# Low parts of the FFN rounds moved from GpSimd to VectorE, and the second pair started chunk by chunk

## Chip, cores, metric

One core of a Trainium2 chip runs the whole kernel. The metric is the device time of one execution in microseconds; the time of a kernel is the median of its runs.

## What is computed

An mLSTM-style attention over 768 steps for 4 batches and 8 heads, then a mixture-of-experts layer in which each expert takes exactly 384 tokens (chosen greedily over all tokens and experts), then a gated FFN on all tokens. Only the second half matters here:

```python
for e in range(E):                      # 8 experts, 384 tokens each
    mask = assigned == e
    h = np.maximum(x[mask] @ w1[e], 0.0)
    out[mask] = h @ w2[e]
...
a = x @ w_a
b = x @ w_b
return (a * b @ w_out).astype(np.float32)
```

## The kernel before

The attention part takes the first 213 us or so; the change doesn't touch it. Then eight **rounds** follow, one for each expert in the order in which experts fill up. A round has 384 tokens (CAP) and two pairs of products.

- **First pair** (`g1`, `g2`): relu(x w1) in eight blocks of 128 features, then times w2. `g2(f-2)` is issued behind `g1(f)`.
- **Second pair** (`ab`, `outp`): for each of twelve blocks two products with w_a and w_b, evacuated by ScalarE (`at`) and multiplied on VectorE (`gf`), then times w_out. `outp(f-2)` is issued behind `ab(f)`.

Every operand is kept as a high and a low part: ScalarE makes the high part by a copy to fp32r (`w1h`, `w2`, `mh`, `xh`, `yh`), another engine subtracts it from the exact value to get the low part (`w1l`, the tail of `w2`, `ml`, `xl`, `yl`), and TensorE takes three products, high by high, low by high, high by low. Before the change GpSimd makes the low parts of the expert's weights (`split_w`, L906, L915, L917; the first two chunks of round 0 are VectorE's) and of the second pair's product (`ml` at L1098), beside gathers of the tokens (`xg`, L845) and scatters of the results (L1137). VectorE makes the low part of the first pair's product (`ml` at L1036), `gf` (L1093), and the low parts of x and y.

Between these the kernel still **routes**: `route(r)` finds expert r's tokens by five counting steps in sequence. A step compares on VectorE (three `G`, L648), counts on TensorE (24 small matmuls into `rt`, L672), tests on VectorE (`okb`, L691), sums on TensorE (L694), and sets the next threshold on VectorE (`d`, L700). Routes 1 to 7 run during rounds 0 to 5 or so. In round 0 five **late conversions** of w_a, w_b and w_out run too (`conv`: VectorE L119, L122, L125, then ScalarE, then GpSimd L134, L136, L149; one buffer `mu`).

What sets the order: each engine works its own list in the order in which the program issues it. The method `mm` adds 0.155 to a counter `now` for every matmul and, when a stream's time has come, takes the next piece of one of three generators: routes, the next expert's weights, late conversions. The number in `yield` is how long that stream then rests on that counter (routes after the first rest 1.25 times as long, PAD). So a VectorE piece is issued a set number of matmuls ahead of the TensorE piece that needs it, and if VectorE is later than that, TensorE stands. In round 0 `wdone` counts the weight steps done, and `g1` pulls the weights stream until enough are.

Of the kernel before, what the change touches and what calls it, by code (L numbers as in the profile page):

```python
# [24 lines left out]
DM = H * D  # L25
E = 8
# [17 lines left out]
class Kern:  # L44
# [68 lines left out]
    def conv(self, pool, kind, i, raw, more, nxt):  # L113
        nc = self.nc
        V, P, A = nc.vector, nc.gpsimd, nc.scalar
        words = raw.bitcast(I32).rearrange("p (n two) -> p n two", two=2)
        qi, sg = self.cva
        u = pool.tile([128, CW], I32, tag="ot", name="mu", bufs=1)
        V.tensor_scalar(u, words[:, :, 1], 3, None, op0=OP.logical_shift_left)  # L119
        more()  # L120
        yield 0.5
        V.tensor_tensor(u, u, qi, op=OP.add)  # L122
        yield 0.8
        F = u.bitcast(F32)
        V.tensor_tensor(F, F, sg, op=OP.mult)  # L125
        if kind == "f":
            h, l = self.wh[i], self.wl[i]
            n4, c4 = slice(0, 512), slice(512, 640)

            def fin():  # L130
                A.activation(h[:, 0:4].rearrange("p a b -> p (a b)"), F[:, n4], AF.Copy)
                th, tl = [pool.tile([128, 128], F32R, name=n, bufs=1) for n in ("mth", "mtl")]
                A.activation(th, F[:, c4], AF.Copy)
                P.tensor_sub(l.rearrange("p a b -> p (a b)"), F[:, n4],  # L134
                             h[:, 0:4].rearrange("p a b -> p (a b)").bitcast(F32))
                P.tensor_sub(tl, F[:, c4], th.bitcast(F32))  # L136
                for s in range(2):
                    r = slice(64 * s, 64 * s + 64)
                    nc.sync.dma_start(h[0:64, 4 + s].bitcast(F32), th[r].bitcast(F32))
                    nc.sync.dma_start(h[64:128, 4 + s].bitcast(F32), tl[r].bitcast(F32))  # L140
                nxt()

            yield from self.later(fin)
        else:
            h = self.woh[i].rearrange("p a b -> p (a b)")

            def fin():
                A.activation(h, F, AF.Copy)
                P.tensor_sub(self.wol[i].rearrange("p a b -> p (a b)"), F, h.bitcast(F32))  # L149
                nxt()  # L150

            yield from self.later(fin)
        self.done.add((kind, i))
# [501 lines left out]
    def route(self, r):  # L655
# [32 lines left out]
        def total(cnt, on):  # L688
            okb = rw.tile([128, E], BF, name="okb")
            ok1 = rw.tile([128, 1], BF, name="ok1")  # L690
            V.tensor_scalar(okb, cnt, float(CAP), None, op0=OP.is_ge, op1=OP.max, accum_out=ok1)  # L691
            yield 0.8
            nn = ps.tile([128, 1], F32, name="rt")
            nc.tensor.matmul(nn, on, ok1, start=True, stop=True)  # L694
            yield 0.6
            return nn
# [198 lines left out]
    def split_w(self, r):  # L895
        nc = self.nc
        V, P, A = nc.vector, nc.gpsimd, nc.scalar

        def one(j):
            raw = self.next_raw()  # L900
            h, l = self.w1h[:, j], self.w1l[:, j]
            A.activation(h, raw, AF.Copy)  # L902
            if r == 0 and j < 2:
                yield 1.0
            e = V if r == 0 and j < 2 else P
            e.tensor_sub(l, raw[:, 0:2], h[:, 0:2].bitcast(F32))  # L906
            V.tensor_sub(h[64:128, 2], raw[64:128, 2], h[64:128, 2].bitcast(F32))  # L907
            self.more_raw()
            yield 2.4

        def two(i):
            raw = self.next_raw()
            h = self.w2[:, 2 * i:2 * i + 2, 0:DM]
            A.activation(h, raw, AF.Copy)
            P.tensor_sub(self.w2[:, 2 * i:2 * i + 2, DM:DM + 64], raw[:, :, 256:320],  # L915
                         h[:, :, 256:320].bitcast(F32))
            P.tensor_sub(self.w2[:, 2 * i:2 * i + 2, DM + 64:], raw[:, :, 0:256], h[:, :, 0:256].bitcast(F32))  # L917
            self.more_raw()
            yield 2.4

        st = [one(j) for j in range(4)] + [two(i) for i in range(NF1 // 2)]
        if r == 0:
            st = [st[i] for i in (0, 1, 4, 2, 5, 3, 6, 7)]
            next(st[0])
            yield 0
            next(st[1])
            yield 0
        for k, f in enumerate(st):
            w = sum(f)
            self.wdone = k + 1  # L930
            yield w

    def prep_x(self, r, xg):
        nc, fw, ps = self.nc, self.fw, self.ps
# [53 lines left out]
    def ffn(self):  # L988
# [34 lines left out]
        for r in range(E):  # L1023
# [15 lines left out]
            def g2(f):  # L1039
                hh, hl = hq.pop(f)  # L1040
                w = self.w2[:, f]
                st, sp = f == 0, f == NF1 - 1
                mm(yp[2], w[:, 256:384], hh, start=st, stop=False)
                mm(yp[2], w[:, 256:384], hl, start=False, stop=sp)
                for m in range(2):
                    wh = w[:, m * 128:m * 128 + 128]
                    wl = w[:, DM + 64 + m * 128:DM + 64 + m * 128 + 128]
                    mm(yp[m], wh, hh, start=st, stop=False)
                    mm(yp[m], wl, hh, start=False, stop=False)
                    mm(yp[m], wh, hl, start=False, stop=sp)  # L1050

            for f in range(NF1):
                while r == 0 and self.wdone < (1, 3, 5, 7)[f // 2] + 1:
# [15 lines left out]
                ws[:] = [self.now, self.weights(r + 1)]  # L1069
            yh = fw.tile([128, 3, CAP], F32R, name="yh", bufs=1)  # L1070
            yl = self.ylt
            yb = fw.tile([64, CAP], F32, tag="at", name="yb", bufs=2)
            A.activation(yb, yp[2][64:128], AF.Copy)
            ys = fw.tile([64, CAP], F32, tag="gf", name="ys", bufs=2)
            V.tensor_add(ys, yp[2][0:64], yb)
            for c in range(2):
                self.split_act(yh, yl, c, yp[c])
            self.split_act(yh, yl, 2, ys)

            gq = {}  # L1080
# [2 lines left out]
            def ab(f):  # L1083
                p = [ps.tile([128, CAP], F32, name="ring", bufs=4) for _ in range(2)]
                wh, wl = self.wh[f], self.wl[f]

                for k in range(2):
                    self.proj(p[k], [wh[:, 2 * k + c] for c in range(2)], [wl[:, 2 * k + c] for c in range(2)],
                              wh[:, 4 + k], yh, yl)
                at = fw.tile([128, CAP], F32, name="at", bufs=2)  # L1090
                A.activation(at, p[0], AF.Copy)  # L1091
                gf = fw.tile([128, CAP], F32, name="gf", bufs=2)
                V.tensor_mul(gf, p[1], at)  # L1093
                gh = fw.tile([128, CAP], F32R, name="mh", bufs=3)
                A.activation(gh, gf, AF.Copy)  # L1095
                gl = fw.tile([128, CAP], F32R, name="ml", bufs=3)
                e = V if r + 1 == E and f == NF2 - 1 else nc.gpsimd
                e.tensor_sub(gl, gf, gh.bitcast(F32))  # L1098
                gq[f] = (gh, gl)

            def outp(f, op, gq, rows=(0, 1, 2)):
# [115 lines left out]
```

## Time and profile before

| | us |
|---|---|
| median of 3 runs | 919.73 (919.49 to 921.26) |
| profiled execution, own time | 922.35 |
| its span, first to last instruction | 920.6 |
| rounds begin (first w1 matmul of each) | 243.0, 347.3, 436.2, 523.1, 608.0, 690.1, 765.1, 838.7 |

| engine | busy us | share of span |
|---|---|---|
| TensorE | 830.0 | 90% |
| VectorE | 543.8 | 59% |
| GpSimd | 433.6 | 47% |
| ScalarE | 337.0 | 37% |

The profile is one execution. Busy times of a stretch are to be read against its own length; the granted clock is that of TensorE, 1.0 being its higher level. "Waits" rows say which instruction stood, and for what.

### The profile page before, as it was taken

The page shows a single profiled execution, that of the slowest core. Times are in us where ns is not written, and L with a number is a line of the kernel's source. Part 1 is how long each engine was busy: PE and PEld are TensorE (multiplying, and loading weights), DVE is VectorE, ACT ScalarE, POOL GpSimd, SP SyncE. Part 2 cuts the span into 40 slices and gives each one's busy share as a digit, 9 for nine tenths or more (in the row PEclk, how much of TensorE's full clock was granted, in tenths as well). Part 3 has the DMA queues.
Part 4 walks back from the last instruction along what each step waited for, and adds up shares of the span by engine and source line. Part 5 has one row for each costly group of instructions (what it writes and reads, how often), then busy time and mean ns, then how long its engine had stood idle before and what let it go on. Part 6 is the DMA issues. An engine that isn't in the chain of part 4 may idle for free.

```text
span 920.6 us, 15838 instructions
## 1 busy us (share of the span) xinstructions
PE 830.0 (90%) x5939; PEld 786.8 (85%) x5939; DVE 543.8 (59%) x1188; ACT 337.0 (37%) x660; POOL 433.6 (47%) x456
## 2 busy tenths in 40 slices
PE   4888978995878889979989999999999999999996
PEld 3788867884778879979988998999899999999996
DVE  7778996846676786585477678667764321321211
ACT  4657646520334332333234224223422532432321
POOL 5688895750433573165147317442723633532122
PEclk9989988896799889989998999999999999999999
DMA  6866765621412220130131022021111311200000
GB/s 170 246 193 198 238 199 143 199 75 41 147 51 72 80 79 22 53 84 13 38 89 45 15 80 75 2 94 32 46 52 43 92 36 43 67 8 22 1 1 22
DMA packets 51037, 73.84 MB, mean 80 GB/s; under 512 B 6160, under 2 KB 41360, under 8 KB 50960
## 3 DMA queue, kind: packets, MB, share of 16 engines
q1 hardware_dynamic: 41744, 45.30, 17.7%
q10 hardware_dynamic: 6912, 19.66, 6.6%
q0 software_dynamic: 2304, 7.87, 2.6%
q8 instruction: 47, 0.77, 0.3%
q14 instruction: 30, 0.25, 0.1%
HBM read 63.37 MB, written 7.86 MB: 77 GB/s over the span
## 4 chain that ended last, share of the span: by engine, by line
PE 64%; DVE 16%; POOL 6%; issue 6%; ACT 5%; DMA 2%; SPq 1%; ACTq 0%; DVEq 0%; POOLq 0%
PE ring L970 32%; PE acc L970 20%; DVE G L648 3%; PE rt L672 2%; PE pq L392 2%; DMA qr<-in_qk_dram 2%; PE pv L423 1%; DVE w1h L907 1%; POOL dd L387 1%; DVE gf L1093 1%; PE pg L408 1%; PE pl L482 1%; DVE mu L122 1%; POOL x L460 1%; ACT yh L966 1%
## 5 line engine op out<-in xcount | busy, mean ns | idle before, releaser
L1098 POOL TENSOR_TENSOR ml<-gf,mh 128x384 fp32r<-128x384 f32 x95 | 106.7, 1123 | 266.4 <-ACT mh L1095 266.1
L970 PE MATMUL ring<-yh,wh 128*128 128x384 f32 x576 | 202.3, 351 | 6.4 <-ACT yh L966 4.6
L970 PE MATMUL ring<-yl,wh 128*128 128x384 f32 x576 | 136.9, 344 | 0.0
L970 PE MATMUL ring<-yh,wl 128*128 128x384 f32 x384 | 132.7, 346 | 0.0
L1093 DVE TENSOR_TENSOR gf<-ring,at 128x384 f32<-128x384 f32 x96 | 53.3, 555 | 126.9 <-PE ring L970 122.8
L970 PEld LDWEIGHTS ring<-yh,wh 128*128 128x128 f32 x576 | 111.4, 193 | 13.9 <-ACT yh L966 7.2
L1095 ACT ACTIVATE mh<-gf 128x384 fp32r<-128x384 f32 x96 | 50.5, 526 | 187.0 <-DVE gf L1093 187.0
L648 DVE TENSOR_TENSOR G<-thc,d 128x1024 bf16<-128x1024 int16 (+1 forms) x90 | 110.4, 1245 | 0.4
L970 PEld LDWEIGHTS ring<-yl,wh 128*128 128x128 f32 x576 | 105.6, 193 | 0.1
L970 PE MATMUL acc<-woh,ml 128*128 128x320 f32 x288 | 91.6, 318 | 0.0
L970 PE MATMUL acc<-woh,mh 128*128 128x320 f32 x288 | 90.7, 315 | 0.0
L970 PE MATMUL acc<-wol,mh 128*128 128x320 f32 x288 | 90.4, 314 | 0.0
L970 PE MATMUL acc<-mh,w 128*128 128x384 f32 x320 | 88.9, 340 | 0.0
L1036 DVE SCALAR_TENSOR_TENSOR ml<-ring,mh 128x384 fp32r<-128x384 f32 x64 | 35.5, 557 | 80.3 <-ACT mh L1034 77.1
L1034 ACT ACTIVATE mh<-ring 128x384 fp32r<-128x384 f32 x64 | 31.5, 492 | 133.5 <-PE ring L970 128.9
L1091 ACT ACTIVATE at<-ring 128x384 f32<-128x384 f32 x96 | 46.8, 488 | 80.0 <-PE ring L970 78.3
L970 PEld LDWEIGHTS ring<-yh,wl 128*128 128x128 f32 x384 | 74.4, 194 | 0.0
L906 POOL TENSOR_TENSOR w1l<-raw,w1h 128x512 fp32r<-128x512 f32 x30 | 44.2, 1478 | 51.0 <-ACT w1h L902 51.0
L970 PE MATMUL ring<-xh,w1h 128*128 128x384 f32 x192 | 66.0, 344 | 0.1
L392 PE MATMUL pq<-qr 128*128 128x256 f32 x192 | 56.9, 425 | 9.9 <-DMA qr<-in_qk_dram 5.2
L970 PE MATMUL acc<-ml,w 128*128 128x384 f32 x192 | 65.2, 339 | 0.3 <-DVE ml L1036 0.3
L970 PEld LDWEIGHTS acc<-mh,w 128*128 128x128 f32 x320 | 58.6, 190 | 0.2 <-issue 0.2
(211 smaller groups left out, 1746.8 us busy)
## 6 DMA issues: line engine op xcount, KB each, us to landing
raw<-in_moe_w_dram SPq DMA_DIRECT2D x32, 320.0 KB
raw<-in_moe_w_dram SPq DMA_DIRECT2D x32, 256.0 KB
vk<-in_vk_dram SPq DMA_DIRECT2D x24, 324.0 KB
qr<-in_qk_dram SPq DMA_DIRECT2D x48, 160.0 KB
mraw<-in_wab_dram ACTq DMA_DIRECT2D x12, 640.0 KB
raw<-in_moe_w_dram SPq DMA_DIRECT2D x64, 64.0 KB
og<-in_og_dram ACTq DMA_DIRECT2D x6, 640.0 KB
qr<-in_qk_dram SPq DMA_DIRECT2D x48, 80.0 KB
```

The lines of the kernel that those rows point to most:

```text
L122: V.tensor_tensor(u, u, qi, op=OP.add)
L392: nc.tensor.matmul(pq[:, o:o + 2], qk[:, 4 + hp], qk[:, H + 2 * hp:H + 2 * hp + 2], start=True, stop=True)
L648: self.nc.vector.tensor_tensor(G, self.thc[:, None, 0:nthr].to_broadcast(dims), d[:, i0:i0 + 8, None].to_broadcast(dims), op=op)
L672: nc.tensor.matmul(cnt[0:nthr], Gs[j][:, i], oh[:, 8 * j + i], start=(j + i == 0), stop=(j * 8 + i == NT - 1))
L906: e.tensor_sub(l, raw[:, 0:2], h[:, 0:2].bitcast(F32))
L970: self.nc.tensor.matmul(*a, **k)
L1034: A.activation(hh, p, AF.Relu)
L1036: V.scalar_tensor_tensor(hl, p, 0.0, hh.bitcast(F32), op0=OP.max, op1=OP.subtract)
L1091: A.activation(at, p[0], AF.Copy)
L1093: V.tensor_mul(gf, p[1], at)
L1095: A.activation(gh, gf, AF.Copy)
L1098: e.tensor_sub(gl, gf, gh.bitcast(F32))
```

## The change

Five edits, in `conv`, `route`, `split_w` and `ffn`:

1. The low parts of w1, w2 and of the second pair's product go from GpSimd to VectorE; those of w2 stand in two pieces with a rest of 1.0 between.
2. In the late conversions (one raw buffer, `rawb == 1`) the multiplication by the sign goes from VectorE to GpSimd.
3. Weight steps are no longer issued whole: `yield from f` replaces `sum(f)`, so `wdone` counts a step one piece later.
4. The rest between `okb` and its sum is 1.2 in place of 0.8.
5. The second pair's start: `g2` makes chunks 0 and 1 of its result ahead of chunk 2, ScalarE and VectorE split chunks 0 and 1 first, and the first block's products go by chunks, both halves interleaved, with the short chunk 2 last.

```diff
-        V.tensor_tensor(F, F, sg, op=OP.mult)
+        (P if self.rawb == 1 else V).tensor_tensor(F, F, sg, op=OP.mult)
...
-            yield 0.8
+            yield 1.2
             nn = ps.tile([128, 1], F32, name="rt")
...
-            e = V if r == 0 and j < 2 else P
-            e.tensor_sub(l, raw[:, 0:2], h[:, 0:2].bitcast(F32))
+            V.tensor_sub(l, raw[:, 0:2], h[:, 0:2].bitcast(F32))
...
-            P.tensor_sub(self.w2[:, 2 * i:2 * i + 2, DM:DM + 64], raw[:, :, 256:320],
+            V.tensor_sub(self.w2[:, 2 * i:2 * i + 2, DM:DM + 64], raw[:, :, 256:320],
                          h[:, :, 256:320].bitcast(F32))
-            P.tensor_sub(self.w2[:, 2 * i:2 * i + 2, DM + 64:], raw[:, :, 0:256], h[:, :, 0:256].bitcast(F32))
+            yield 1.0
+            V.tensor_sub(self.w2[:, 2 * i:2 * i + 2, DM + 64:], raw[:, :, 0:256], h[:, :, 0:256].bitcast(F32))
...
-            yield 2.4
+            yield 1.4
...
-            w = sum(f)
+            yield from f
             self.wdone = k + 1
-            yield w
...
-                mm(yp[2], w[:, 256:384], hh, start=st, stop=False)
-                mm(yp[2], w[:, 256:384], hl, start=False, stop=sp)
                 for m in range(2):
...
+                mm(yp[2], w[:, 256:384], hh, start=st, stop=False)
+                mm(yp[2], w[:, 256:384], hl, start=False, stop=sp)
...
+            for c in range(2):
+                self.split_act(yh, yl, c, yp[c])
             yb = fw.tile([64, CAP], F32, tag="at", name="yb", bufs=2)
...
-            for c in range(2):
-                self.split_act(yh, yl, c, yp[c])
             self.split_act(yh, yl, 2, ys)
...
-                for k in range(2):
+                if f == 0:
+                    for c in range(2):
+                        for k in range(2):
+                            mm(p[k], wh[:, 2 * k + c], yh[:, c], start=c == 0, stop=False)
+                            mm(p[k], wl[:, 2 * k + c], yh[:, c], start=False, stop=False)
+                    for c in range(2):
+                        for k in range(2):
+                            mm(p[k], wh[:, 2 * k + c], yl[:, c], start=False, stop=False)
+                    for k in range(2):
+                        mm(p[k], wh[:, 4 + k], yh[:, 2], start=False, stop=False)
+                    for k in range(2):
+                        mm(p[k], wh[:, 4 + k], yl[:, 2], start=False, stop=True)
+                for k in range(2 if f else 0):
...
-                e = V if r + 1 == E and f == NF2 - 1 else nc.gpsimd
-                e.tensor_sub(gl, gf, gh.bitcast(F32))
+                V.tensor_sub(gl, gf, gh.bitcast(F32))
```

VectorE, late in round 0's second pair, around the first counting step of route 2, before (`ta`, `tb`, `k` are small threshold sums, `d` the threshold, `G` the comparison):

```order
L1093 TENSOR_TENSOR gf<-ring,at 128x384
L710 TENSOR_SCALAR ta<-k_3659 128x24
L711 TENSOR_SCALAR tb<-k_3659 128x24
L691 TENSOR_SCALAR okb,ok_3834<-rt 128x8
L700 TENSOR_SCALAR d_3857<-ta,rt 128x24
L704 SCALAR_TENSOR_TENSOR k_3783<-rt,tb 128x24
L648 TENSOR_TENSOR G<-thc,d_3857 128x1024
L1093 TENSOR_TENSOR gf<-ring,at 128x384
```

The same place on VectorE now (w_2440 is the tile `w2`):

```order
L710 TENSOR_SCALAR ta<-k_3667 128x24
L711 TENSOR_SCALAR tb<-k_3667 128x24
L691 TENSOR_SCALAR okb,ok_3844<-rt 128x8
L914 TENSOR_TENSOR w_2440<-raw_3726,w_2440 128x2x64
L917 TENSOR_TENSOR w_2440<-raw_3726,w_2440 128x2x256
L1104 TENSOR_TENSOR gf<-ring,at 128x384
L1108 TENSOR_TENSOR ml<-gf,mh 128x384
L700 TENSOR_SCALAR d_3876<-ta,rt 128x24
L704 SCALAR_TENSOR_TENSOR k_3799<-rt,tb 128x24
L648 TENSOR_TENSOR G<-thc,d_3876 128x1024
```

Between `okb` and `d` there now stand two weight pieces and a `gf` with its `ml` right behind it.

GpSimd in round 0, from the last weight pieces to the second gather, before:

```order
L917 TENSOR_TENSOR w_2440<-raw_2880,w_2440 128x2x256
L134 TENSOR_TENSOR wl_2426<-mu,wh_2425 128x512
L136 TENSOR_TENSOR mtl<-mu,mth 128x128
L149 TENSOR_TENSOR wol_2432<-mu,woh_2431 128x640
L1098 TENSOR_TENSOR ml<-gf,mh 128x384 x3
L134 TENSOR_TENSOR wl_2428<-mu,wh_2427 128x512
```

And now, from the first gather on:

```order
L845 DMA xg<-xd,idx 128x320 x3
L125 TENSOR_TENSOR mu<-mu,msg 128x640
L134 TENSOR_TENSOR wl_2426<-mu,wh_2425 128x512
L136 TENSOR_TENSOR mtl<-mu,mth 128x128
L125 TENSOR_TENSOR mu<-mu,msg 128x640
L149 TENSOR_TENSOR wol_2432<-mu,woh_2431 128x640
L125 TENSOR_TENSOR mu<-mu,msg 128x640
```

The conversions' multiplications (L125) came in; after the five conversions GpSimd holds gathers, scatters and one-element memsets alone.

TensorE where the second pair of round 1 starts, before (chunks are not named: the first five `yh` rows are chunk 0, 0, 1, 1, 2 of one half):

```order
L970 MATMUL acc<-ml,w_2440 128x384
L970 MATMUL ring<-yh,wh_69 128x384
L970 MATMUL ring<-yh,wl_70 128x384
L970 MATMUL ring<-yh,wh_69 128x384
L970 MATMUL ring<-yh,wl_70 128x384
L970 MATMUL ring<-yh,wh_69 128x384
L970 MATMUL ring<-yl,wh_69 128x384 x3
```

And now, from the third of four such `yh` pairs on:

```order
L969 MATMUL ring<-yh,wh_69 128x384
L969 MATMUL ring<-yh,wl_70 128x384
L969 MATMUL ring<-yh,wh_69 128x384
L969 MATMUL ring<-yh,wl_70 128x384
L969 MATMUL ring<-yl,wh_69 128x384 x4
L969 MATMUL ring<-yh,wh_69 128x384 x2
L969 MATMUL ring<-yl,wh_69 128x384 x2
```

Chunk 2 was the fifth matmul behind the last `acc`; now it is the thirteenth.

## Rows read from the trace of the kernel before

**Rows 1.** Busy time by stretch, one per round (0 to 4, then 6); last columns clock, DMA

```profile
243.00:347.30 104.30, 88.93 (x630) 84.12 (x629) 80.92 (x154) 40.40 (x74) 53.77 (x45) 0.89 0.24 72
347.30:436.20 88.90, 82.94 (x615) 78.81 (x615) 58.87 (x124) 27.70 (x54) 35.27 (x35) 0.96 0.15 45
436.20:523.10 86.90, 82.39 (x616) 78.75 (x615) 58.14 (x118) 26.17 (x51) 35.71 (x33) 0.96 0.15 46
523.10:608.00 84.90, 82.03 (x617) 78.34 (x617) 55.50 (x123) 26.52 (x51) 36.53 (x33) 0.98 0.17 51
608.00:690.10 82.10, 80.00 (x614) 76.63 (x614) 58.69 (x123) 26.06 (x51) 37.49 (x33) 1.00 0.19 59
...
765.10:838.70 73.60, 73.21 (x438) 72.23 (x438) 17.43 (x32) 26.41 (x51) 30.66 (x33) 1.00 0.12 37
```

**Rows 2.** What TensorE waited for in rounds 1 to 4: total us, times, longest

```profile
PE rt L672 <- DVE G L648: 8.6, 6, 3.0
PE rt L694 <- DVE okb L691: 4.7, 4, 2.1
PE ring L970 <- ACT yh L966: 1.5, 4, 0.5
```

**Rows 3.** The same for round 0

```profile
PE rt L672 <- DVE G L648: 8.8, 5, 4.2
PE rt L740 <- DVE ok L737: 2.7, 1, 2.7
```

**Rows 4.** VectorE by time: start us, duration; one operation in rounds 0 and 1, one successor

```profile
320.12 0.35 DVE L629 TENSOR_TENSOR e<-e,w 128x192 f32<-128x192 f32 x1
320.38 0.17 DVE L630 TENSOR_SCALAR d<-sg 128x24 int32<-128x24 int32 x1
...
395.89 4.22 DVE L629 TENSOR_TENSOR e<-e,w 128x192 f32<-128x192 f32 x1
```

**Rows 5.** GpSimd by time, around the second of these

```profile
396.37 1.03 POOL L1098 TENSOR_TENSOR ml<-gf,mh 128x384 fp32r<-128x384 f32 x1
397.34 2.54 POOL L906 TENSOR_TENSOR w1l<-raw,w1h 128x512 fp32r<-128x512 f32 x2
```

**Rows 6.** VectorE's groups by shape in round 1: busy us, mean ns, idle before

```profile
L648 DVE TENSOR_TENSOR G<-thc,d 128x1024 bf16<-128x1024 int16 x15 | 20.0, 1336 | 0.0
...
L648 DVE TENSOR_TENSOR G<-thc,rr 128x1024 bf16<-128x1024 int16 x3 | 3.6, 1218 | 0.0
...
L907 DVE TENSOR_TENSOR w1h<-raw,w1h 64x256 fp32r<-64x256 f32 x4 | 2.5, 618 | 2.1 <-ACT w1h L902 2.0
...
L710 DVE TENSOR_SCALAR ta<-k 128x24 int32<-128x24 int32 x1 | 1.2, 1210 | 0.0
...
L711 DVE TENSOR_SCALAR tb<-k 128x24 int32<-128x24 int32 x1 | 0.2, 165 | 0.0
```

**Rows 7.** VectorE's groups from 232 to 245 us, GpSimd idle: moved operations' prices

```profile
L906 DVE TENSOR_TENSOR w1l<-raw,w1h 128x512 fp32r<-128x512 f32 x2 | 1.4, 692 | 0.7 <-ACT w1h L902 0.7
...
L907 DVE TENSOR_TENSOR w1h<-raw,w1h 64x256 fp32r<-64x256 f32 x2 | 0.8, 423 | 0.1
```

**Rows 8.** VectorE by time at the end, where it makes one `ml` itself

```profile
910.20 0.56 DVE L1098 TENSOR_TENSOR ml<-gf,mh 128x384 fp32r<-128x384 f32 x1 [0.59 <-ACT mh L1095]
```

**Rows 9.** Chain of work that ended last: one counting step's 24 matmuls

```profile
344.36 0.60 PE rt L672 x24
```

**Rows 10.** All engines by time where round 6's second pair starts

```profile
788.32 1.02 ACT L962 ACTIVATE yh<-acc 128x384 fp32r<-128x384 f32 x2
...
788.47 0.34 PE L970 MATMUL acc<-ml,w 128*128 128x384 f32 x1
...
790.34 0.44 PE L970 MATMUL ring<-yh,wh 128*128 128x384 f32 x1 [0.33 <-ACT yh L966]
```

**Rows 11.** GpSimd and VectorE by time in round 0's conversions

```profile
280.28 1.56 POOL L149 TENSOR_TENSOR wol<-mu,woh 128x640 fp32r<-128x640 f32 x1 [9.09 <-ACT woh L148]
...
295.55 0.50 DVE L119 TENSOR_SCALAR mu<-mraw 128x640 int32<-128x640 int32 x1 [3.19 <-POOL mtl L136]
```

## The prediction

> **What bounds the kernel now.** I read the busy time by round first [rows 1]. TensorE works 73.21 of 73.60 us in round 6, where no routing is left: that is a round's floor. Rounds 0 to 4, in which routes run, take 104.3, 88.9, 86.9, 84.9 and 82.1 us. The four from 1 to 4 sum to 342.8, which is 48.4 over four floors. Of that 17.5 is honest work: seven sets of 24 counting matmuls a round at 0.60 to 0.65 [rows 9]. TensorE's own waits in these rounds are 8.6 us for `G` and 4.7 us for `okb` [rows 2], both VectorE's; 1.5 us is the second pair's start. The granted clock was 0.96, 0.96 and 0.98 in rounds 1 to 3 [rows 1], which is 3.6 + 3.5 + 1.7 = 8.8 us lost. About 7 us are left over in shorter waits. Round 0 has 8.8 us of waits for `G`, 2.7 for `ok` [rows 3], and a clock of 0.89, some 11.5 us lost [rows 1]. So the routes' comparisons on VectorE end last, though VectorE is busy only 55 to 59 us of these rounds.
>
> Why they are late is in the single operations. The same multiplication takes 0.35 us in round 0 and 4.22 us in round 1 [rows 4]; through the second, GpSimd worked three instructions in a row, from 396.37 to 399.88 [rows 5]. In round 1, fifteen `G` average 1336 ns where three others average 1218, a small `ta` takes 1210 where its neighbour `tb` takes 165, and `w1h` 618 [rows 6] where it takes 423 with GpSimd idle [rows 7]. That makes 15 x 0.12 = 1.8, 3.9, 1.0 and 0.8 us; taking every shape of round 1 in this way I get 10.0 us of VectorE time lost to GpSimd, 10 to 11 in rounds 2 to 4, 19.5 in round 0.
>
> **The change, part by part.**
>
> *Moved to VectorE.* Per round: twelve `ml` at 0.56 [rows 8], 6.7 us; four `w1l` at 0.69 [rows 7], 2.8 us; four large pieces of w2 of the same 512 elements, 2.8 us; four of 128 elements, which the trace lacks: between the 0.17 of a 24-element operation [rows 6] and the 0.42 of 256 [rows 7], I take 0.29, 1.2 us (0.7 to 1.7). Sum 13.4. Beside it, `ml` stands directly behind its `gf`, and ScalarE's copy lies between: VectorE stood 0.59 us there in the one instance there is [rows 8]. Twelve times that is 7.1. So VectorE gets 20.5 us a round and gives back 10: from 58.9 to about 69 in round 1. That fits a round of 78 on the whole, but not evenly. In round 1's third to eleventh `ab` I count 90 VectorE operations worth 42.6 us by these prices; with nine waits of 0.59 that is 47.9; successive operations overlap by 0.09 (one starts 0.26 after a 0.35 us one [rows 4]), which takes off some 6.5: 41.4. TensorE has 25 matmuls a step at a mean of 73.21/438 = 0.167 [rows 1], 4.2 us, nine times that is 37.6, and four counting sets of 0.65 more, 40.2. So VectorE is over by 1 us in round 1's second pair and about even in the next three; but unevenly: a step with three `G`, a `gf`/`ml` pair and two pieces of w2 asks 6.4 us of it, against 4.2 + 0.65. I take 2.0, 1.2, 0.5 and 0.3 us of waits from that in rounds 1 to 4. Besides, `ok` and the scan of `place` are issued only about half a microsecond to one ahead of their TensorE consumers; with a `gf`/`ml` pair (0.56 + 0.59) in front, each round waits there for about 1 us in all. New waits in rounds 1 to 4: 3.0 + 2.2 + 1.5 + 1.3 = 8 us, between 0 and 40 (the rivals below). Waits that short, spread out, I take to leave the clock alone, as round 4's did: it was 1.00 with TensorE busy 80.0 of 82.1 us [rows 1]. So rounds 1 to 4 win 13.3 + 8.8 - 8 = 14.
>
> Is the exchange worth anything? Against it stands the small `ta` at 1210 ns beside `tb` at 165 [rows 6]: with GpSimd at work a small operation can take seven times as long, and this goes with the subtractions. The Trainium skill ("Perfetto Trace Analysis", Optimizing Scalar/DVE Operations) warns that moving work between GpSimd and VectorE might not help, since they share a read port. By that this part and round 0's would sum to 0 and the time to about 917; by the rows they are 14 and 8. It is a rival below.
>
> *GpSimd without subtractions.* Its list loses what stood before the gathers and scatters; they start sooner. I cost this at nothing: a gather has most of a second pair before it is needed. If that cover were gone, a round would begin later by what a gather takes to land; no row of the rounds has TensorE waiting for one [rows 2, 3].
>
> *Round 0.* Of the 8.8 us of waits for `G` most goes, since its longest (4.2 [rows 3]) stands behind one stretched operation, and about 5 of the 11.5 us of clock. Against that: the conversions' five multiplications on GpSimd read two inputs of 128x640, like the subtraction of 1.56 [rows 11]. They lie in the conversion's chain (VectorE, GpSimd, ScalarE, GpSimd, then the next conversion on the same buffer), for which VectorE already stood 3.19 once [rows 11]; VectorE saves about 0.83 each (0.69 and 128 elements more at 1.05 ns, the slope between the two of rows 7). GpSimd is busy 16 us in place of 53.8 [rows 1] in round 0, so by proportion 6 of the 19.5 us of contention stay. VectorE's list there is full (80.9 of 104.3 before [rows 1]). I take 6 us of new waits, between 0 and 16. Net: 8.8 + 5.0 + 0.5 for the pair's start (below) - 6 = 8.
>
> *Second pair's start.* In round 6 the last `acc` starts at 788.47 and the fifth product, chunk 2's, at 790.34; five at 0.167 would bring it at 789.31 [rows 1, 10]: 1.0 us lost. Now chunk 2's ScalarE steps come behind those of chunks 0 and 1, which start about 0.5 us sooner, and twelve matmuls (2.1 us) cover it. The copies of chunk 0 and 1 take 1.02 [rows 10], then 0.5, 0.55 and 1.0 for chunk 2: ready some 2.5 us after the last `acc`. So 0.5 us a round stays and 0.5 goes: 2 us in rounds 1 to 4 and 1.5 in 5 to 7. One counting set moves from round 4's end into round 5 or so: 0.6 back.
>
> *Rests.* 1.2 for 0.8 makes each route 2 longer on the counter; routes have over a round of slack, so nothing. Issuing weight steps in pieces adds no work; in round 0 it brings one half step forward ahead of `g1`, 0.7 us of VectorE, in the 6 above.
>
> Sum: 14 + 2 + 8 + 1.5 - 0.6 = 25 us off the profiled execution's own time of 922.35 (span 920.6): 897.4. The median is 2.6 below that execution, so **895**.
>
> **Rivals.**
>
> *Full relief.* VectorE keeps up everywhere and the clock stays up: rounds 1 to 4 win 22.1 + 2, round 0 8.8 + 2.7 + 0.5 + 9 of its clock, the rest 1: 46, time 874. For it: VectorE has 78 - 69 = 9 us free in a round. Against it: the counted surplus in the second pairs.
>
> *VectorE becomes the bound, slower.* Every route has seven links in which TensorE needs a VectorE result at once (four `okb`, `ok`, the scan, `pos`). If each stands behind a `gf`/`ml` pair, 1.15 us, that is 8 us a round in five rounds, 40 in place of the 14 that I took: the gain is gone. If the clock falls again as in round 1, four times 3.6 come on top: 934. It decides from 40 us of new waits. For it: VectorE works in order, and both its added load and its waits lie in the same second pairs. Against it: `okb` now gets half as much rest again.
>
> *No change.* VectorE pays 20.5 us a round and gets 10 back, and TensorE's waits for it only change places, from `G` behind stretched operations to `okb` and `ml` behind ScalarE; of the 2.9 us of the pair starts one is lost in the same way: 918. Against it: VectorE's busy time of before leaves a third of rounds 1 to 4 free [rows 1]. This is what the page's warning would come to here.
>
> **How the numbers follow.** Forecast 0.72, full relief 0.12, slower 0.10, no change 0.06. The predicted time is the forecast's. The range goes from 874, full relief's own value, to 918, no change's; it leaves out half of each of the two and the slower case, 0.19. Differences under 0.2% (1.8 us) this kernel's runs can't tell from none: faster 0.85, within 0.2% 0.05, slower 0.10.
>
> **What would show it.** VectorE's `ta` and `k` near 0.17 and all `G` near 1.22 from round 1 on; GpSimd idle but for gathers there; rounds 1 to 4 at 80 to 83, round 0 near 96, round 6 at 73.1. TensorE's waits for `G` and `okb` shorter, many under 1 us. Wrong if waits over 2 us stay in rounds 1 to 4, if the clock is below 0.95 there, or if `ml` waits for ScalarE much longer than 0.6.

## The result, and the profile after

The changed kernel takes 911.91 us (median of 4 runs, 910.85 to 913.58) beside 919.75 for the kernel before: a ratio of 0.9916, 95% interval 0.9893 to 0.9938. It is faster, by 7.8 us where 25 were forecast. The profiled execution takes 911.54 us (span 909.8), 10.8 less than the one before; the medians differ by less, since the profiled execution before lay 2.6 above its median.

Busy time by round after, to be read against [rows 1]: stretch, its length, then TensorE, its weight loads, VectorE, ScalarE, GpSimd, and at the end clock, DMA share and GB/s.

```profile
242.20:342.00 99.80, 85.62 (x606) 80.76 (x604) 78.29 (x175) 39.93 (x73) 22.34 (x17) 0.94 0.25 76
342.00:427.30 85.30, 82.02 (x614) 78.09 (x615) 60.08 (x147) 27.15 (x53) 7.29 (x9) 0.98 0.16 46
427.30:512.10 84.80, 81.17 (x615) 78.36 (x614) 59.23 (x145) 26.59 (x52) 6.32 (x9) 0.98 0.16 47
512.10:595.80 83.70, 80.92 (x616) 78.18 (x615) 57.59 (x141) 26.13 (x51) 6.27 (x9) 0.98 0.16 47
595.80:680.30 84.50, 80.79 (x618) 77.22 (x617) 57.02 (x146) 26.25 (x51) 6.25 (x9) 1.00 0.17 51
...
755.20:828.30 73.10, 72.78 (x438) 72.33 (x438) 29.81 (x56) 26.49 (x51) 6.11 (x9) 1.00 0.13 38
```

Rounds 1 to 4 sum to 338.3 us, 4.5 less than before. A round splits into three parts that these rows give at once: TensorE idle (length less its busy time), clock lost (length times what the clock lacks of 1.0), and the rest, TensorE's work at full clock.

| rounds 1 to 4, us | sum | idle | clock lost | work |
|---|---|---|---|---|
| before [rows 1] | 342.8 | 15.4 | 8.8 | 318.6 |
| forecast | 326.8 | 8.2 | 0 | 318.6 |
| after | 338.3 | 13.4 | 5.1 | 319.8 |

So the gain that is missing there, 11.5 us, is idle time (5.2), clock (5.1) and 1.2 of work. (The clock is given to two decimals, so what it cost is known to some 0.4 us a round, and so is the work.) Round 0 came from 104.3 to 99.8, forecast was 96.

What the move was meant to bring did come. VectorE's groups in round 1 after, beside [rows 6] (busy us, mean ns, idle before):

```profile
L648 DVE TENSOR_TENSOR G<-thc,d 128x1024 bf16<-128x1024 int16 x15 | 18.3, 1219 | 0.0
...
L1108 DVE TENSOR_TENSOR ml<-gf,mh 128x384 fp32r<-128x384 f32 x11 | 6.1, 558 | 6.5 <-ACT mh L1106 6.5
...
L905 DVE TENSOR_TENSOR w1l<-raw,w1h 128x512 fp32r<-128x512 f32 x4 | 2.7, 686 | 0.2 <-issue 0.2
...
L914 DVE TENSOR_TENSOR w<-raw,w 128x128 fp32r<-128x128 f32 x6 | 1.7, 286 | 0.0
L906 DVE TENSOR_TENSOR w1h<-raw,w1h 64x256 fp32r<-64x256 f32 x4 | 1.7, 422 | 0.1
...
L710 DVE TENSOR_SCALAR ta<-k 128x24 int32<-128x24 int32 x1 | 0.2, 179 | 0.0
```

`G` fell from 1336 to 1219 ns, `w1h` from 618 to 422, `ta` from 1210 to 179. The price is in `ml`'s row: 6.1 us of work in round 1 and, in its last column, 6.5 us in which VectorE stood for ScalarE's copy `mh`, 0.59 each time. What TensorE still waits for in rounds 1 to 4, beside [rows 2] (total us, times, longest):

```profile
PE rt L672 <- DVE G L648: 6.6, 5, 2.0
PE rt L784 <- DVE z L756: 2.7, 3, 1.1
PE rt L694 <- DVE okb L691: 2.1, 2, 1.6
```

These three come to 11.4 us, all of them for VectorE (`z` is what the scan of `place` works on). One of these waits in round 3, VectorE first and then TensorE (start us, duration, in brackets the idle time ahead of it and who ended it):

```profile
550.22 0.42 DVE L906 TENSOR_TENSOR w1h<-raw,w1h 64x256 fp32r<-64x256 f32 x1
550.68 0.56 DVE L1104 TENSOR_TENSOR gf<-ring,at 128x384 f32<-128x384 f32 x1
551.82 0.56 DVE L1108 TENSOR_TENSOR ml<-gf,mh 128x384 fp32r<-128x384 f32 x1 [0.59 <-ACT mh L1106]
552.30 1.22 DVE L648 TENSOR_TENSOR G<-thc,d 128x1024 bf16<-128x1024 int16 x1
553.43 0.68 DVE L905 TENSOR_TENSOR w1l<-raw,w1h 128x512 fp32r<-128x512 f32 x1
554.15 0.42 DVE L906 TENSOR_TENSOR w1h<-raw,w1h 64x256 fp32r<-64x256 f32 x1
554.60 1.23 DVE L648 TENSOR_TENSOR G<-thc,d 128x1024 bf16<-128x1024 int16 x1
```

```profile
553.58 0.35 PE L672 MATMUL rt<-oh,G 128*128 128x8 bf16 x8 [0.83 <-DVE G L648]
555.89 0.35 PE L672 MATMUL rt<-oh,G 128*128 128x8 bf16 x8 [1.96 <-DVE G L648]
```

Nothing is stretched any more; VectorE is behind, and yet between `gf`'s end (551.23) and 551.82 it does nothing, with `G` ready to go behind `ml`. TensorE pays with 0.83 and 1.96. Of these 2.8 us the standing is 0.59; the rest is the other work in the list, `gf` and `ml` ahead of the second `G`, two weight pieces ahead of the third.

### The profile page after: what moved, and what is told of

It is laid out like the page before. It is cut to its first block, busy times and chain, and to the rows that moved or that the text cites. A ratio compares the mean times of both kernels' runs of the same rounds, so it can differ in the third digit from the quotient of the medians.

```text
span 909.8 us, 15808 instructions
## 1 busy us (share of the span) xinstructions
PE 825.8 (91%) x5939; PEld 785.2 (86%) x5939; DVE 582.6 (64%) x1372; ACT 336.3 (37%) x660; POOL 222.7 (24%) x272
## 3 DMA queue, kind: packets, MB, share of 16 engines
q1 hardware_dynamic: 41744, 45.30, 17.9%
## 4 chain that ended last, share of the span: by engine, by line
PE 50%; DVE 21%; issue 13%; DMA 5%; ACT 5%; POOL 5%; SPq 1%; ACTq 0%; POOLq 0%; DVEq 0%
PE ring L969 26%; PE acc L969 15%; DVE G L648 3%; PE rt L672 2%; DMA mraw<-in_wab_dram 2%; DMA qr<-in_qk_dram 2%; PE pq L392 2%; DVE gf L1104 2%; ACT mh L1106 1%; DVE mu L122 1%; DMA vk<-in_vk_dram 1%; DVE ml L1108 1%; PE pv L423 1%; DVE w1l L905 1%; PE pg L408 1%
## 5 line engine op out<-in xcount | busy, mean ns | idle before, releaser
L969 PE MATMUL ring<-yh,wh 128*128 128x384 f32 x576 | 197.6, 345 | 2.9 <-ACT yh L965 2.8
L1147 POOL DMA_INDIRECT out_dram<-ot,idx x24 | 25.9, 1080 | 418.3 <-ACT ot L1145 414.9
L969 PEld LDWEIGHTS ring<-yh,wh 128*128 128x128 f32 x576 | 109.5, 191 | 5.4 <-ACT yh L965 4.7
L648 DVE TENSOR_TENSOR G<-thc,d 128x1024 bf16<-128x1024 int16 (+1 forms) x90 | 93.2, 1048 | 0.4
L1108 DVE TENSOR_TENSOR ml<-gf,mh 128x384 fp32r<-128x384 f32 x96 | 53.8, 560 | 56.8 <-ACT mh L1106 55.6
L392 PE MATMUL pq<-qr 128*128 128x256 f32 x192 | 59.1, 437 | 8.6 <-DMA qr<-in_qk_dram 6.2
L845 POOL DMA_INDIRECT xg<-xd,idx x24 | 24.0, 1000 | 149.0 <-PE ring L969 67.2
```

The source lines that it names most:

```text
L392: nc.tensor.matmul(pq[:, o:o + 2], qk[:, 4 + hp], qk[:, H + 2 * hp:H + 2 * hp + 2], start=True, stop=True)
L648: self.nc.vector.tensor_tensor(G, self.thc[:, None, 0:nthr].to_broadcast(dims), d[:, i0:i0 + 8, None].to_broadcast(dims), op=op)
L845: self.nc.gpsimd.indirect_dma_start(out=xg[:, t], out_offset=None, in_=self.xd, in_offset=bass.IndirectOffsetOnAxis(ap=self.idx[r][:, t:t ...
L969: self.nc.tensor.matmul(*a, **k)
L1108: V.tensor_sub(gl, gf, gh.bitcast(F32))
L1147: st = nc.gpsimd.indirect_dma_start(out=self.out, out_offset=bass.IndirectOffsetOnAxis(ap=self.idx[r][:, t:t + 1], axis=0), in_=ot[:, t], ...
```

## The experiments

Three theories. **A**: VectorE's own list is what is late, A1 by `ml`'s standing wait for ScalarE, A2 by the work added to it. **B**: the links of a route are issued too near to the TensorE work that needs them. **C**: time lost to GpSimd's work beside it decides. All kernels were timed against the kernel before (919.6 to 920.5 on those chips).

| kernel | median us (range) | ratio, 95% interval | rounds 0 to 4 | idle, r1–4 | clock lost, r1–4 |
|---|---|---|---|---|---|
| changed kernel | 911.9 (910.9–913.6) | 0.9916 (0.9893–0.9938) | 438.1 | 13.4 | 5.1 |
| 1 `ml` on GpSimd | 901.1 (896.6–906.9) | 0.9816 (0.9771–0.9862) | 426.4 | 10.6 | 1.7 |
| 2 weights on GpSimd | 923.5 (920.2–928.4) | 1.0041 (1.0015–1.0066) | 454.3 | 22.7 | 10.5 |
| 3 old start | 910.4 (905.3–912.8) | 0.9904 (0.9868–0.9940) | 436.2 | | |
| 4 no `ml` | 887.0 (885.0–888.6) | 0.9650 (0.9615–0.9686) | 414.1 | 4.4 | 0 |
| 5 no low parts | 881.7 (879.6–885.9) | 0.9591 (0.9551–0.9631) | 407.6 | 2.4 | 0 |
| 6 `ml` later | 900.7 (899.9–903.3) | 0.9792 (0.9753–0.9831) | 428.2 | 10.5 | 1.7 |
| 7 `ml` without its wait | 892.8 (890.5–897.6) | 0.9709 (0.9671–0.9748) | 423.1 | 7.2 | 1.6 |
| 8 weights' edit alone | 909.4 (907.2–912.5) | 0.9882 (0.9845–0.9918) | 435.7 | 11.1 | 5.1 |
| 9 both pairs' `ml` later | 899.2 (895.5–901.1) | 0.9788 (0.9740–0.9836) | 427.3 | 9.6 | 1.7 |
| 10 conversions on VectorE | 911.5 (907.4–916.1) | 0.9911 (0.9879–0.9943) | 441.5 | | |
| 11 `okb` rest 0.8 | 914.8 (910.4–919.8) | 0.9951 (0.9919–0.9983) | 443.5 | | |
| 12 as 9, `G` earlier | 902.7 (900.4–907.7) | 0.9829 (0.9793–0.9864) | 427.8 | 11.1 | 5.1 |

The last three columns are of one profiled execution each. In it the rounds began between 236.3 and 242.4 us, though hardly any edit reaches what runs ahead of them (tiles cleared in 4, 5 and 7, some first weight pieces); so rounds are compared first and totals second. Rounds scatter too: kernel 10's edit does not reach rounds 1 to 4, and these took 340.3 us there, 2.0 more than in the changed kernel.

**1. `ml` back on GpSimd.**

```diff
-                V.tensor_sub(gl, gf, gh.bitcast(F32))
+                e = V if r + 1 == E and f == NF2 - 1 else nc.gpsimd
+                e.tensor_sub(gl, gf, gh.bitcast(F32))
```

> The changed kernel (911.9 us) with the second pair's low part ml made by GpSimd again; the weights' low parts stay on VectorE. Theory A (what VectorE got in its ordered list, above all ml with its wait of 0.6 us for ScalarE, makes TensorE stand at the routes' links): VectorE loses twelve times 0.56 + 0.6 = 13.8 us a round and gets back the contention of ml, some 4 us a round; the waits for okb, the scan and G in rounds 1 to 4 fall from 20 us to about 10, time 900 to 906. Theory B (the links are issued too near to their consumers, whatever VectorE holds): no change, 910 to 914. Theory C (time lost to GpSimd is what costs, and the move of ml is what won): rounds 1 to 4 go half of the way back to before, 914 to 918.

Undoing this part of the move wins 10.8 us, as theory A said. GpSimd's and VectorE's groups in its round 1:

```profile
L1109 POOL TENSOR_TENSOR ml<-gf,mh 128x384 fp32r<-128x384 f32 x11 | 12.5, 1135 | 52.8 <-ACT mh L1106 52.8
```

```profile
L648 DVE TENSOR_TENSOR G<-thc,d 128x1024 bf16<-128x1024 int16 x14 | 17.0, 1218 | 0.0
...
L905 DVE TENSOR_TENSOR w1l<-raw,w1h 128x512 fp32r<-128x512 f32 x4 | 4.3, 1086 | 1.5 <-ACT w1h L902 1.5
...
L914 DVE TENSOR_TENSOR w<-raw,w 128x128 fp32r<-128x128 f32 x6 | 3.8, 627 | 1.2 <-ACT w L913 1.2
...
L710 DVE TENSOR_SCALAR ta<-k 128x24 int32<-128x24 int32 x1 | 0.2, 178 | 0.0
```

Eleven `ml` of 1135 ns on GpSimd, and those `G` and `ta` stay at 1218 and 178 ns. Others were stretched: `w1l` from 686 to 1086, the small pieces of w2 from 286 to 627, the three `G` of token places from 1220 to 1492, one `me` from 228 to 1039. That is some 5 us of VectorE time in this round, where `ml` on VectorE takes 6.1 of work and 6.5 of standing. So `ml` on GpSimd contends too, and it is still the cheaper place. C can't account for what the changed kernel still loses: in its round 1 nothing is stretched.

**2. The weights' low parts back on GpSimd, `ml` on VectorE.**

```diff
-            V.tensor_sub(l, raw[:, 0:2], h[:, 0:2].bitcast(F32))
+            e = V if r == 0 and j < 2 else P
+            e.tensor_sub(l, raw[:, 0:2], h[:, 0:2].bitcast(F32))
...
-            V.tensor_sub(self.w2[:, 2 * i:2 * i + 2, DM:DM + 64], raw[:, :, 256:320],
+            P.tensor_sub(self.w2[:, 2 * i:2 * i + 2, DM:DM + 64], raw[:, :, 256:320],
...
-            V.tensor_sub(self.w2[:, 2 * i:2 * i + 2, DM + 64:], raw[:, :, 0:256], h[:, :, 0:256].bitcast(F32))
+            P.tensor_sub(self.w2[:, 2 * i:2 * i + 2, DM + 64:], raw[:, :, 0:256], h[:, :, 0:256].bitcast(F32))
```

> The changed kernel with the weights' low parts made by GpSimd again; ml stays on VectorE. VectorE loses 6.7 us a round and gets back contention of the weights, some 6 us a round in long pieces of up to 4 us. Theory A: those cancel, 910 to 915, as ml is the costlier move. Theory B: 910 to 914. Theory C: the long waits for G (2 to 4 us) and the clock falls behind them come back, 915 to 920.

Slower than before by 0.15 to 0.66%, and above the figures of all three theories. VectorE's groups in its round 1, then TensorE's longest item of waits in rounds 1 to 4:

```profile
L648 DVE TENSOR_TENSOR G<-thc,d 128x1024 bf16<-128x1024 int16 x14 | 19.5, 1401 | 0.0
...
L907 DVE TENSOR_TENSOR w1h<-raw,w1h 64x256 fp32r<-64x256 f32 x4 | 2.6, 660 | 0.3 <-ACT w1h L902 0.2
...
L710 DVE TENSOR_SCALAR ta<-k 128x24 int32<-128x24 int32 x1 | 1.2, 1226 | 0.0
```

```profile
PE rt L672 <- DVE G L648: 16.5, 8, 3.3
```

The stretched `G`, `w1h` and `ta` of [rows 6] are back with the weights alone. With one `e` of 2993 ns (359 in the changed kernel) VectorE loses some 8 us in this round. So C names the right loss of the kernel before, and the weights' pieces alone are enough for it.

**3. The old start of the second pair**: edit 5 of the change undone.

```diff
-            for c in range(2):
-                self.split_act(yh, yl, c, yp[c])
             yb = fw.tile([64, CAP], F32, tag="at", name="yb", bufs=2)
...
+            for c in range(2):
+                self.split_act(yh, yl, c, yp[c])
             self.split_act(yh, yl, 2, ys)
...
-                for k in range(2 if f else 0):
+                for k in range(2):
```

> The changed kernel with the second pair's start as before (chunk 2 first, first block by halves). All theories: 0.4 us a round as round 6 shows (73.6 to 73.2), so 3 to 4 us slower, 915 to 916; if the start stands behind VectorE's list in rounds 0 to 4 more than in round 6, up to 920.

No difference in the total, where 3 to 4 us were expected, and none in rounds 1 to 4 (336.2 us, 338.3 with the new start). It shows in the rounds with few or no routes: round 6 takes 73.6 us, with the new start 73.1 to 73.2.

**4. No `ml` in the second pair**, a zeros tile in its place.

```diff
-                gl = fw.tile([128, CAP], F32R, name="ml", bufs=3)
-                V.tensor_sub(gl, gf, gh.bitcast(F32))
+                gl = self.nol
```

> The changed kernel without the subtraction for ml in the second pair: its low part is a tile of zeros, TensorE's work is the same. VectorE loses 13.8 us a round and GpSimd gets nothing. Theory A: rounds 0 to 4 lose most of their 20 + 12 us of waits, 890 to 900. Theory B: 908 to 912. Theory C says nothing of it, since no contention changes: 911.

It wins 24.9 us, more than A's figure: TensorE's idle time in rounds 1 to 4 falls from 13.4 to 4.4 us and the clock stays at 1.00.

**5. As 4, and no low parts of the weights** (`w1l`, the tail of `w2`).

```diff
-            V.tensor_sub(l, raw[:, 0:2], h[:, 0:2].bitcast(F32))
...
-            V.tensor_sub(self.w2[:, 2 * i:2 * i + 2, DM:DM + 64], raw[:, :, 256:320],
-                         h[:, :, 256:320].bitcast(F32))
...
-            V.tensor_sub(self.w2[:, 2 * i:2 * i + 2, DM + 64:], raw[:, :, 0:256], h[:, :, 0:256].bitcast(F32))
```

> The changed kernel without ml's subtraction in the second pair and without the weights' low parts on any engine (tiles of zeros stand in; TensorE's work is the same): neither added load on VectorE nor contention, but for the late conversions. It is the ceiling of the exchange, the full relief of 874 in the prediction. If the routes' own links still make TensorE stand (theory B), it stays near e4 without ml (887), 883 to 887. If VectorE's load alone makes the waits (theory A), rounds 1 to 4 come down to 78 to 79 each and round 0 to about 85: 870 to 878.

It lies between A's figure and B's. Its rounds 1 to 4 are what is left when VectorE is hardly ever late:

```profile
328.39:408.11 79.72, 79.44 (x614) 76.65 (x614) 47.20 (x119) 27.52 (x53) 7.30 (x9) 1.00 0.17 50
408.11:488.50 80.39, 79.17 (x615) 76.68 (x614) 48.10 (x121) 27.28 (x52) 6.18 (x9) 1.00 0.17 49
488.50:567.54 79.04, 79.04 (x615) 76.64 (x614) 44.75 (x116) 26.61 (x51) 6.12 (x9) 1.00 0.17 50
567.54:648.46 80.92, 79.98 (x617) 76.77 (x616) 45.05 (x121) 26.59 (x51) 6.23 (x9) 1.00 0.17 51
```

TensorE works 317.6 us in them at a clock of 1.00, 25 more than four rounds of 73.1. So this edit could not have brought a routed round under 79 to 80 us.

**6. The second pair's `ml` six matmuls later**, so that ScalarE's copy is done when VectorE gets to it, the same work otherwise.

```diff
-                V.tensor_sub(gl, gf, gh.bitcast(F32))
+                low[f] = lambda: V.tensor_sub(gl, gf, gh.bitcast(F32))
...
-                    outp(f - 2, op, gq)
+                    outp(f - 2, op, gq, (0, 1))
+                    low.pop(f)()
+                    outp(f - 2, op, gq, (2,))
+                else:
+                    low.pop(f)()
```

> The changed kernel with ml's subtraction still on VectorE, but issued six matmuls later than its gf (ahead of the third row of the w_out products), so that other pieces can stand between and ScalarE's copy is done by then; same work. Theory A1 (the standing wait of 0.6 us for ScalarE in VectorE's ordered list costs most of the 25 us by which ml on VectorE is dearer than no ml): 897 to 903. Theory A2 (ml's occupancy of 0.56 us costs it): 909 to 913.

This is A1's experiment, and it wins 11.3 us with nothing taken off VectorE. VectorE in its round 2: here `ml` comes five operations behind `gf`, with no bracket.

```profile
478.24 0.56 DVE L1104 TENSOR_TENSOR gf<-ring,at 128x384 f32<-128x384 f32 x1
478.72 0.23 DVE L700 TENSOR_SCALAR d<-ta,rt 128x24 int16<-128x24 int32 x1
478.86 0.17 DVE L704 SCALAR_TENSOR_TENSOR k<-rt,tb 128x24 int32<-128x24 f32 x1
478.98 1.23 DVE L648 TENSOR_TENSOR G<-thc,d 128x1024 bf16<-128x1024 int16 x1
480.12 0.28 DVE L914 TENSOR_TENSOR w<-raw,w 128x128 fp32r<-128x128 f32 x1
480.32 0.55 DVE L1108 TENSOR_TENSOR ml<-gf,mh 128x384 fp32r<-128x384 f32 x1
```

VectorE's stands for `mh` in rounds 0 to 4, in the changed kernel and in this one (total us, times, longest):

```profile
DVE ml L1108 <- ACT mh L1106: 34.3, 58, 0.6
```

```profile
DVE ml L1108 <- ACT mh L1106: 16.4, 29, 0.6
```

17.9 us less standing made rounds 0 to 4 9.9 us shorter. Of the 60 `ml`, 28 still come directly behind their `gf` and stand as before: the first two blocks of each second pair, and those for which the program had nothing else to issue between.

**7. `ml` in its old place, but subtracting a ready tile**: the same length of work on VectorE, no wait.

```diff
-                V.tensor_sub(gl, gf, gh.bitcast(F32))
+                V.tensor_sub(gl, gf, self.nol.bitcast(F32))
```

> The changed kernel with ml's subtraction on VectorE at the same place, but taking away a tile of zeros that has long been there in place of ScalarE's copy: the occupancy of 0.56 us without the wait; the low part is therefore wrong by the high part, TensorE's work is the same. Theory A1 (the wait): 892 to 900. Theory A2 (occupancy): 907 to 912.

`ml` is unchanged at 558 ns in round 1 and stands 0.4 us in all, where it stood 6.5 (this kernel leaves out taking away the high part, so its low part is wrong; TensorE's work is the same):

```profile
L1110 DVE TENSOR_TENSOR ml<-gf,nol 128x384 fp32r<-128x384 f32 x11 | 6.1, 558 | 0.4
```

```profile
331.20:413.29 82.09, 80.29 (x613) 76.73 (x614) 59.74 (x145) 27.20 (x53) 7.26 (x9) 1.00 0.17 48
413.29:494.94 81.65, 79.46 (x616) 76.81 (x614) 60.34 (x146) 26.84 (x52) 6.69 (x9) 1.00 0.16 49
494.94:576.93 81.99, 80.72 (x615) 78.09 (x614) 57.56 (x140) 26.26 (x51) 6.46 (x9) 0.98 0.17 48
576.93:659.36 82.43, 80.46 (x618) 77.02 (x617) 57.33 (x145) 26.35 (x51) 6.24 (x9) 1.00 0.18 52
```

With 4 this splits what `ml` on VectorE costs: by rounds 0 to 4, 24.0 us, of which 15.0 are the wait and 9.0 the work; by the medians 24.9, of which 19.1 and 5.9. The rounds are the better measure: the profiled execution of kernel 7 is 21.0 us shorter than the changed kernel's, and 5.9 of that lie ahead of round 0. The wait is clear of noise; the work less so, since the intervals of 4 and 7 overlap a little.

**8. The kernel before with the weights' edit alone**: low parts on VectorE, in pieces.

```diff
-            e = V if r == 0 and j < 2 else P
-            e.tensor_sub(l, raw[:, 0:2], h[:, 0:2].bitcast(F32))
+            V.tensor_sub(l, raw[:, 0:2], h[:, 0:2].bitcast(F32))
...
-            P.tensor_sub(self.w2[:, 2 * i:2 * i + 2, DM + 64:], raw[:, :, 0:256], h[:, :, 0:256].bitcast(F32))
+            yield 1.0
+            V.tensor_sub(self.w2[:, 2 * i:2 * i + 2, DM + 64:], raw[:, :, 0:256], h[:, :, 0:256].bitcast(F32))
...
-            w = sum(f)
+            yield from f
```

> The kernel before with only the weights' low parts moved to VectorE and issued in pieces: ml stays on GpSimd, the conversions' multiplication on VectorE, the second pair's start and the okb rest as before. If the weights' move is the part that won (it is what e1 and e2 differ in), 900 to 908; if it needs the conversions' move, the longer rest and the new start beside it, 912 to 918.

It gives as much as the five edits together. Kernel 1, which has the weights and the small edits but not `ml`, gains 8.3 more than this one, in intervals that overlap a little.

**9. As 6, and the first pair's `ml` three matmuls later.**

```diff
-                V.scalar_tensor_tensor(hl, p, 0.0, hh.bitcast(F32), op0=OP.max, op1=OP.subtract)
+                hlow[f] = lambda: V.scalar_tensor_tensor(hl, p, 0.0, hh.bitcast(F32), op0=OP.max, op1=OP.subtract)
...
                 for m in range(2):
+                    if m and f + 2 in hlow:
+                        hlow.pop(f + 2)()
```

> The kernel with ml issued six matmuls late (900.7 us) and the same done in the first pair: its ml is issued three matmuls into the w2 products instead of directly behind its ScalarE copy. VectorE stood 30.7 us there in rounds 1 to 4, in 22 waits. If those waits cost as the second pair's did (theory A1 for every low part in VectorE's list), 893 to 898. If they cost nothing, because VectorE is ahead of TensorE there and has nothing else to do, 899 to 903.

No difference from 6 that can be measured. VectorE's stands in the first pairs of rounds 0 to 4, in the changed kernel and in this one:

```profile
DVE ml L1035 <- ACT mh L1033: 33.7, 24, 3.0
```

```profile
DVE ml L1035 <- ACT mh L1033: 32.1, 25, 2.6
```

They hardly fell by issuing `ml` later: VectorE is ahead there, stands up to 3 us and has nothing else to do. Since the standing stayed, this run does not show what it costs; kernel 4 does. There VectorE stands 39.2 us for the first pair's `mh` in rounds 1 to 4, and TensorE is idle 4.4 in all. A row of standing as large as the second pair's is thus by itself no sign of a loss; it is one where work that others need is queued behind.

**10. The conversions' multiplication back on VectorE**, and **11. the rest behind `okb` 0.8 again.**

```diff
-        (P if self.rawb == 1 else V).tensor_tensor(F, F, sg, op=OP.mult)
+        V.tensor_tensor(F, F, sg, op=OP.mult)
```

> The changed kernel with the late conversions' multiplication on VectorE again. Only round 0 can change. If the multiplication on GpSimd lengthens the conversion's chain (VectorE stood 1.6 us for it, and contention with GpSimd stays), round 0 gets shorter by 1 to 4 us: 908 to 911. If VectorE's list is what is full in round 0 (five times 0.82 us), round 0 gets longer by 1 to 4: 913 to 916.

```diff
-            yield 1.2
+            yield 0.8
             nn = ps.tile([128, 1], F32, name="rt")
```

> The changed kernel with the rest behind okb at 0.8 as before. Theory B (links issued too near to their consumers): TensorE's waits for okb grow by 0.4 x 1.25 x 1.05 = 0.5 us at each of four links a route, up to 2 us a round, 915 to 922. Theory A (VectorE is seconds late, not tenths): little, 911 to 914.

10 changes nothing that can be told from the scatter. 11 costs 2.9 us, in intervals that overlap a little, and 5.4 in rounds 0 to 4: that points to a small gain of the longer rest, and so to a part for B, but is not clear of noise. (The "seconds" and "tenths" of 11's expectation are of microseconds.)

**12. As 9, with the rest between `G` and its 24 matmuls 1.7 in place of 1.0.**

```diff
             if r:
-                yield 1.0
+                yield 1.7
                 for j in range(3):
                     mms(j)
```

> The version with both low parts late, and in routes 1 to 6 the rest between the last comparison G and its 24 counting matmuls is 1.7 in place of 1.0 (times 1.25 from route 2 on). With both low parts late TensorE still waited for G 5.2 us in round 0 and 1.4, 2.1, 2.2 and 0 us in rounds 1 to 4. Theory B (what is left is that these links are issued too near to their consumers): these waits and the clock lost behind them go, round 0 comes to about 92, rounds 1 to 4 to 80 to 82, the time to 888 to 892. Theory A2 (what is left is VectorE's occupancy, its list being behind by more than the rest): the wait moves to okb, ok and the scan behind it, the time stays at 897 to 901. If it gets over 903, the longer rests push routes into rounds that had none.

The edit was made in both places where a route has this rest, the counting steps and `place`. B's figure did not come. What TensorE waits for in rounds 0 to 4 in kernel 9, and in this one:

```profile
PE rt L672 <- DVE G L648: 11.0, 8, 2.2
...
PE rt L694 <- DVE okb L691: 2.5, 3, 1.6
```

```profile
PE rt L694 <- DVE okb L691: 11.9, 9, 2.6
...
PE rt L672 <- DVE G L648: 2.5, 4, 0.8
```

The waits for `G` went over to `okb`, one link on.

Round 5 grew from 74.9 to 79.1 us since routes now reach into it. What is left after 9 is thus not one link's short lead. That VectorE's list is behind by more than a longer rest at one place can cover, A2, fits this, though the time lies just over A2's figure; longer rests at both links were not tried, so A2 is not shown against B.

Four versions that leave nothing out beat both kernels: 1, 6, 9 and 12, at 899 to 903 us. Their intervals overlap, so none of them is named the best.

## Why the prediction was right in direction and wrong in size

**The contention: right.** `G` at 1219, `ta` at 179, GpSimd idle but for gathers and scatters from round 1 on, as said. What the forecast did not do is price the two parts apart: in round 1 `ml` on GpSimd costs VectorE some 5 us (1) and the weights' pieces some 8 (2), while on VectorE `ml` takes 12.6.

**Prices on VectorE: right.** `ml` 558 ns for 0.56, `w1l` 686 for 0.69, the small pieces of w2 286 for the 0.29 that was taken between two bounds, the wait 0.59 each, 6.5 us in round 1 for the 7.1 of twelve.

**The step that failed: "New waits in rounds 1 to 4: ... 8 us", and the clock put at nothing.** Its prices held, but not what it made of them: TensorE's waits for VectorE came to 11.4 us there, and the clock lost 5.1. I weighed VectorE's load against TensorE's time over nine blocks and took the small surplus as the loss. The 0.59 of standing was in that load, but as an average, as if the free time around it could absorb it. It can't where a route's link stands directly behind: the list is worked in order, and the links come every few us. Kernel 7 shows the size: without the standing wait rounds 1 to 4 come to 328.2 us (its rows above), 1.4 from the 326.8 of the forecast; with it they take 338.3. The wait alone is worth 10.1 us there, 6.2 of it idle time and 3.5 clock. In other words the forecast was about right for a kernel in which `ml` waits for nothing; that the two agree so closely is in part luck, since kernel 7 still loses 1.6 us of clock where the forecast has none. The sentence that waits so short leave the clock alone was wrong too: it was 0.98 in rounds 1 to 3 after. None of the forecast's three signs of being wrong came: the longest wait of rounds 1 to 4 was 1.96 us, the clock never below 0.95, the standing 0.6. They looked for long waits, and what stayed was ten for VectorE of 1.1 us on average.

**Round 0: the same step.** 99.8 for a forecast of 96; kernel 7 has 94.93. Its clock gave 5.5 us (0.89 to 0.94) where 5 were taken; idle time fell only from 15.4 to 14.2, and TensorE's work at full clock rose by some 2 us, for which no run gives the reason. The conversions, for which new waits were feared, cost nothing that 10 could tell from the scatter, though GpSimd's five multiplications took 2.05 us each where the nearest row has 1.56, and GpSimd was busy 22.3 us where 16 were taken.

**"About 7 us are left over in shorter waits": wrong, without effect on the sum.** Length less busy time in [rows 1] is 15.4 us for rounds 1 to 4, and [rows 2] accounts for 14.8 of it. There was no room for 7 more. It is TensorE's own work: 25 us over the floor in kernel 5 where I had 17.5.

**The pair's start: right in rounds 5 to 7, not seen in 1 to 4.** Against kernel 3 it gains 0.5 us in each of rounds 5 to 7, and nothing that shows in rounds 1 to 4, for which 2 us were taken. In round 6 after, TensorE's last `acc`, the first new product and the thirteenth:

```profile
778.56 0.34 PE L969 MATMUL acc<-ml,w 128*128 128x384 f32 x1
778.73 0.34 PE L969 MATMUL ring<-yh,wh 128*128 128x384 f32 x1
...
781.32 0.62 PE L969 MATMUL ring<-yh,wh 128*128 128x384 f32 x2 [0.32 <-ACT yh L965]
```

Twelve products at 0.173 would bring the thirteenth at 780.81: 0.5 us lost, as said, and 73.6 became 73.1.

**The rivals.** "VectorE becomes the bound" described the mechanism that was at work, links behind a `gf`/`ml` pair of 1.15 us; it didn't reach 40 us. "No change" had the page "Perfetto Trace Analysis" of the Trainium skill (Optimizing Scalar/DVE Operations) beside it: moving work between GpSimd and VectorE might not help. The runs give both answers: moving the weights alone helped (8: 0.9882), moving `ml` without the weights, with the small edits, hurt (2: 1.0041), and the two together gave a third of what was expected.

**Open.** Why kernel 1 gains 8.3 us over kernel 8. The longer rest (some 3 us in 11) and the new start (0.5 a round where no routes run, 3) may be part of it; neither was taken out with `ml` on GpSimd.

## What to carry to other kernels

On an engine that works a list in order, an operation whose operand comes from another engine should not be issued directly behind the operation that starts that engine, if work that others need stands behind it: issue it a few operations later, when the operand is ready. Ask of a moved operation not only what it takes but where the engine will stand for it, and what is queued behind; here the standing was worth some 15 us and the work some 9. Before calling a rest "short waits", take length less busy time: it says how much waiting there can be.

## What was not expected of the hardware

- Which `G` were stretched went by which engine had started first. In rounds 1 to 4 of kernel 2, 22 of the 128x1024 `G` overlap a weights' piece on GpSimd: the 17 that started behind it took 1.37 to 2.32 us, the 5 that started ahead of it about 1.22. In kernel 1, 21 overlap an `ml` on GpSimd: 4 started behind it and took 2.03 or 2.04, 17 ahead of it about 1.22. So `ml` leaves the `G` alone for the most part because most of them are already running when it starts.
- About half of the standing in VectorE's second pairs came out as time: 34.3 us of it in rounds 0 to 4 were worth 15.0 there (7), 17.9 of it 9.9 (6).
- The clock doesn't follow the idle time alone: kernel 6's round 2 has 4.0 us idle (length 83.75, busy 79.71) at 1.00, the changed kernel's round 3 has 2.8 at 0.98 (its two waits, 0.83 and 1.96, are those shown above) and its round 4 has 3.7 at 1.00.
